# When the values of a head pair are loaded: with its first head into two buffers, or with its second into one

## The chip, the cores and the metric

The kernel runs on one core of one Trainium2 chip. The metric is the device time of one execution in microseconds (us), and the figure that counts is the median of several executions.

## The reference, cut to what matters

Causal attention with a decay, followed by two MLPs. Four batches (B), eight heads (H), 576 positions (S), head size 64.

```python
def _attn_ref(q, k, v, f):
    log_f = np.log(np.clip(f, 0.0001, 1.0))
    cum = np.cumsum(log_f, axis=-1)
    decay = cum[:, :, :, None] - cum[:, :, None, :]
    scores = scale * np.matmul(q, k.transpose(0, 1, 3, 2))
    scores = np.where(causal, -1000000000.0, scores + decay)
    attn = np.exp(scores - np.max(scores, axis=-1, keepdims=True))
    attn = attn / (np.sum(attn, axis=-1, keepdims=True) + 1e-09)
    return np.matmul(attn, v)

x = attn_out.transpose(0, 2, 1, 3).reshape(B, S, H * D)
x = _moe_ref(x)    # layer norm, x + relu(xn @ w_ch1) @ w_ch2
out = _moe2_ref(x) # relu(x @ w_in), gate with w_spatial, @ w_out
```

## The kernel before

The positions are cut by query: queries 0 to 127 of all batches first, then 128 to 255, then 256 to 575 one batch at a time. This last kind is what the change touches: the method `attention`, called four times (batches 0 to 3), each call working through four pairs of heads (p = 0 to 3), each pair through its two heads (u = 0, 1). So there are 16 pairs, counted here 0 to 15 through the four batches. Beside this attention runs the first MLP on what earlier blocks of queries gave (lines L849 and L864, the two products of a group of 256 or 512 tokens); both share TensorE, ScalarE and VectorE. A group of the MLP starts when the attention and the norm of its block are done.

What a pair does, in the order in which the code writes it:

- `operands` (L325) for the head after the present one: on SyncE's queue a load of that head's q and k (`qk`, 448 KB, L330, three buffers) and of its decay rows (`x2z`, L338); then ScalarE and VectorE split the operands in two parts (L319, L341, L342).
- with the second head (`if u`, L608): the load of the pair's v for both heads (`vr`, 320 KB, L610), on SyncE's queue too, into one buffer (`BUFS["vr"]` is 1).
- `weights` (L344) for query tiles 2 and 3 of each head: scores on TensorE (L359), masked minimum on VectorE (L363), exponentials on ScalarE (L367), the weights in two fp16 parts (`P16`, L319 and L380), and their transposition by a DMA on SyncE's queue (L382).
- after both heads: `weights` for the last tile of both, then `parts16` (L265): `vr` becomes two fp16 parts `vp` (two buffers), a high one on ScalarE (L280) and a low one on VectorE (L281). This is called the cast below; with its end the buffer of `vr` is free.
- `values` (L578), one pair late: the transposed weights times `vp` (L586), put into `xT` and `xt` on ScalarE (L591, L592). It frees the buffer of `vp`.

At the end of a batch `xT` is stored to memory by a DMA that ScalarE's queue issues (L1347), and the norm of that block begins with the subtraction of the mean in place (L782).

The code does not run in the order in which it is written. A planner orders each engine's instructions and each queue's DMAs when the kernel is compiled: what is written earlier goes first, but where an engine would have nothing to do, the planner takes a later instruction whose inputs and buffers are there by its own estimate of the times. On the chip each queue then runs in that order; an instruction that waits holds everything behind it on its queue. The transpositions and the loads of `qk`, `x2z`, `vr` and of the MLP's raw weights are all on SyncE's one queue (SPq in the rows).

Of the kernel before, what the change touches and what calls it, by code (L numbers as in the profile page):

```python
# [25 lines left out]
TOK = 256  # L26
QW = S - 2 * P
SC = 2.0 ** 14
BUFS = dict(vr=1, vp=2, qk=3, x1=3, x2=3, PT=4, sd=3, st=6, P16=5, xt=1)
BUFS0 = dict(vr=1, qk=1, e=4, diag=2, PT=2, st=4)  # L30
BUFS1B = dict(vr=4, vp=4, qk=4, sd=4, P16=4, PT=3, st=8)
BUFS1 = dict(vr=3, vp=3, qk=3, sd=2, P16=2, PT=2, st=6)
# [43 lines left out]
def qtile(i):  # L76
    return i * P, min(S, (i + 1) * P)
# [11 lines left out]
class Kernel:  # L89
# [235 lines left out]
    def operands(self, bh):  # L325

        nc, at = self.nc, self.at
        W, C = QW, QW + S
        qk = at.tile([P, C], F32, tag="qk", name="qk", bufs=BUFS["qk"])
        nc.sync.dma_start(out=qk, in_=self.qk[bh // H, bh % H])  # L330
        x1 = at.tile([P, C], F32R, tag="x1", name="x1", bufs=BUFS["x1"])
        if not self.x2z:
            for i in range(BUFS["x2"]):
                self.x2z.append(at.tile([P, C], F32R, name=f"x2z{i}"))
# [10 lines left out]
    def weights(self, i, heads):  # L345

        nc, at, bufs, q0 = self.nc, self.at, BUFS, 2 * P
        lo, hi = qtile(i)
# [222 lines left out]
    def attention(self, b, xT, xt, middle=None):  # L571
        nc, at, bufs = self.nc, self.at, BUFS
        q0, W = 2 * P, QW
        stored = xt is None
        if stored:
            xt = at.tile([P, NP, S - 512], F32, tag="xt", name="xt", bufs=bufs["xt"])

        def values(p, vp, vsc, heads, behind=None):  # L578

            pav = self.bank("av")  # L580
            for kt in range(5):
                n0 = max(kt * P, q0) - q0
                for vi, pi in ((0, 1), (1, 0), (0, 0)):
                    for u in range(2):
                        us = slice(64 * u, 64 * u + 64)
                        ins = nc.tensor.matmul(  # L586
                            pav[us, n0:W], lhsT=vp[:, vi, kt, us], rhs=heads[u][1][:, 2 * kt + pi, n0:W],
                            start=(kt == 0 and (vi, pi) == (0, 1)), stop=(kt == 4 and (vi, pi) == (0, 0)), skip_group_check=True)
                        if behind is not None and kt == 0 and (vi, pi) == (0, 1):
                            self.after(ins, behind)  # L590
            nc.scalar.activation(xT[:, p, :], pav[:, :TOK], AF.Copy, scale=vsc)  # L591
            nc.scalar.activation(xt[:, p, :], pav[:, TOK:W], AF.Copy, scale=vsc)  # L592
            if p == 1:
                self.xs = self.mo_sum(xT)
            elif p == 2:
                nc.vector.tensor_tensor(out=self.xs, in0=self.xs, in1=xT[:, 2, :], op=ALU.add)

        late = None
        passes = self.operands(b * H)
        for p in range(NP):  # L600
            if middle and p == 2:
                middle()
            heads = []
            for u in range(2):
                heads.append((passes, at.tile([P, 10, W], F16, tag="PT", name="PT", bufs=bufs["PT"])))
                if 2 * p + u + 1 < H:
                    passes = self.operands(b * H + 2 * p + u + 1)
                if u:  # L608
                    vr = at.tile([P, 5, P], F32, tag="vr", name="vr", bufs=bufs["vr"])
                    nc.sync.dma_start(out=vr, in_=self.v[b, :, p * P : (p + 1) * P].rearrange("(t p) d -> p t d", p=P))  # L610
                yield
                for i in (2, 3):
                    done = self.weights(i, heads[u:])
                    if late and (u, i) == (1, 3):
                        yield
                        values(*late, done)
                    yield
            vp = at.tile([P, 2, 5, P], F16, tag="vp", name="vp", bufs=bufs["vp"])
            self.weights(4, heads)
            vsc = self.parts16(vr, vp[:, 0], vp[:, 1], b)  # L620
            late = p, vp, vsc, heads
            yield
        yield
        values(*late)
        yield
        if stored:
            nc.scalar.dma_start(out=self.xt_d[:, :, b, :], in_=xt)
        return self.xs
# [905 lines left out]
```

## Time and profile before

| what | value |
|---|---|
| median of 3 executions | 764.3 us (762.98 to 765.41) |
| the profiled execution | 763.16 us, its span 761.2 us |
| TensorE busy in the span | 739.7 us (97%) |
| VectorE, ScalarE busy | 590.9 us (78%), 528.8 us (69%) |
| granted TensorE clock | 1.000 (2.4 GHz) |
| load of `vr` of queries from 256 on | 16 times, 320 KB each, issued between 191.7 and 427.7 us |

The span runs from the first to the last instruction of the profile; the 2.0 us between it and the time of the same execution lie around it. All stretches are counted from the start of the span.

### The profile page before, as it was taken

To read this page: it belongs to the slowest core of one execution; us is meant where nothing else is said; L and a number is where in the kernel's file an instruction comes from. 1 tells how busy PE (TensorE), PEld (TensorE's weight loads), DVE (VectorE), ACT (ScalarE), POOL (GpSimd) and SP (SyncE) were. 2 spreads that over 40 slices of the span, in tenths; PEclk is the share of its full clock that TensorE was granted. 3 is DMA by queue.
4 is the path that set the end of the run, shared out by engine and by line. 5 is a ranking of instruction groups with operands and counts; after the bars stand their busy time and mean duration, and the time that the engine had idled before them with its cause. 6 is when DMAs were issued, how large, how long until landed. Compare 5 with 4: busy or idle time off the path is not lost.

```text
span 761.2 us, 16265 instructions
## 1 busy us (share of the span) xinstructions
PE 739.7 (97%) x5912; PEld 567.9 (75%) x5912; DVE 590.9 (78%) x1569; ACT 528.8 (69%) x1320; POOL 67.4 (9%) x102
## 2 busy tenths in 40 slices
PE   8899998999999999999999999999999999999998
PEld 6788887888888877877888888644447678768686
DVE  7899799577599989989869845689456796785854
ACT  6898699576588989879857844587346764664633
POOL 6001100013102010110110100200012000000000
PEclk9999999999999999999999999999999999999999
DMA  8978694466589998988965944831025240100101
GB/s 263 295 269 274 206 266 84 89 171 105 176 167 206 198 220 183 195 189 177 201 144 116 148 84 149 213 132 56 1 22 111 70 125 1 44 21 7 57 2 62
DMA packets 164100, 104.68 MB, mean 138 GB/s; under 512 B 106147, under 2 KB 151299, under 8 KB 164021
## 3 DMA queue, kind: packets, MB, share of 16 engines
q1 hardware_dynamic: 153032, 93.06, 50.3%
q0 software_dynamic: 5376, 5.54, 5.2%
q10 hardware_dynamic: 5612, 5.06, 2.2%
q8 instruction: 46, 0.75, 0.4%
q14 instruction: 34, 0.27, 0.1%
HBM read 64.37 MB, written 15.11 MB: 104 GB/s over the span
## 4 chain that ended last, share of the span: by engine, by line
PE 63%; DVE 11%; ACT 10%; DMA 10%; issue 4%; SPq 2%; DVEq 0%; ACTq 0%
PE ph L864 16%; PE acc L849 12%; PE pb L808 8%; PE pb L809 8%; PE pb L810 8%; DMA raw<-in_moe_w_ch_dram 3%; PE s L359 3%; PE s L849 3%; DMA vr<-in_v_dram 2%; PE av L586 2%; ACT wt L744 2%; ACT P L319 2%; DMA x_d<-xT 2%; DVE P L380 1%; DMA qk<-decay 1%
## 5 line engine op out<-in xcount | busy, mean ns | idle before, releaser
L849 PE MATMUL acc<-hh,wt 128*128 128x256 f16 (+2 forms) x960 | 196.8, 295 | 3.2 <-ACT hh L875 3.2
L864 PE MATMUL ph<-xh,wt 128*128 128x256 f16 (+1 forms) x896 | 185.0, 288 | 2.0 <-DVE hl L879 2.0
L864 PEld LDWEIGHTS <-wt 128*128 128x128 f16 x1344 | 126.9, 98 | 47.4 <-issue 10.2
L849 PEld LDWEIGHTS <-wt 128*128 128x128 f16 x1344 | 128.7, 98 | 44.3 <-issue 5.3
L864 PE MATMUL ph<-xl,wt 128*128 128x256 f16 (+1 forms) x448 | 129.0, 288 | 0.0
L849 PE MATMUL acc<-hl,wt 128*128 128x256 f16 (+1 forms) x416 | 115.8, 281 | 1.1 <-DVE hl L879 1.1
L875 ACT ACTIVATE hh<-ph 128x256 f16<-128x256 f32 (+2 forms) x128 | 50.9, 397 | 45.8 <-PE ph L864 45.5
L879 DVE SCALAR_TENSOR_TENSOR hl<-ph,hh 128x256 f16<-128x256 f32 (+1 forms) x112 | 50.5, 453 | 35.9 <-ACT hh L875 35.7
L319 ACT ACTIVATE P<-sd,st 128x512 f16<-128x512 f32 (+2 forms) x128 | 70.6, 585 | 9.8 <-DVE st L370 6.9
L380 DVE SCALAR_TENSOR_TENSOR P<-sd,st,P 128x384 f16<-128x384 f32 (+2 forms) x96 | 59.2, 634 | 10.5 <-ACT P L319 10.3
L367 ACT ACTIVATE sd<-sd,st 128x384 f32<-128x384 f32 (+2 forms) x80 | 54.6, 682 | 14.4 <-DVE st L363 14.2
L359 PE MATMUL s<-x2z 128*128 128x384 f32 (+3 forms) x128 | 47.8, 382 | 1.9 <-DMA x2z<-decay_d 1.7
L363 DVE CUSTOM_DVE_ANT_0 sd<-s,mask 128x384 f32<-128x384 f32 (+2 forms) x80 | 46.0, 579 | 3.7 <-PE s L359 2.7
L900 POOL DMA_DIRECT2D x_d<-t x36 | 31.9, 1024 | 182.7 <-DVE t L896 153.1
L359 PE MATMUL s<-x 128*128 128x384 f32 (+3 forms) x128 | 41.4, 333 | 0.0
L809 PE MATMUL pb<-wsl,vh 128*128 128x288 f16 x128 | 36.6, 286 | 0.0
L808 PE MATMUL pb<-wsh,vl 128*128 128x288 f16 x128 | 36.6, 286 | 0.0
L810 PE MATMUL pb<-wsh,vh 128*128 128x288 f16 x128 | 36.4, 286 | 0.0
L810 PE MATMUL pb<-gh,woh 128*128 128x288 f16 x128 | 35.0, 286 | 0.0
L809 PE MATMUL pb<-gl,woh 128*128 128x288 f16 x128 | 35.0, 286 | 0.0
L808 PE MATMUL pb<-gh,wol 128*128 128x288 f16 x128 | 33.3, 286 | 0.0
L922 ACT ACTIVATE gh<-u 128x288 f16<-128x288 f32 x32 | 14.0, 437 | 26.5 <-DVE u L1261 26.5
(341 smaller groups left out, 1692.5 us busy)
## 6 DMA issues: line engine op xcount, KB each, us to landing
raw<-in_moe_w_ch_dram SPq DMA_DIRECT2D x32, 512.0 KB
qk<-in_qk_dram SPq DMA_DIRECT2D x32, 448.0 KB
vraw<-in_v_dram SPq DMA_DIRECT2D x5, 1024.0 KB
vr<-in_v_dram SPq DMA_DIRECT2D x16, 320.0 KB
x_d<-t POOLq DMA_DIRECT2D x36, 128.0 KB, 4.3
out_dram<-o SPq DMA_DIRECT2D x32, 144.0 KB
raw<-in_moe_w_in_dram SPq DMA_DIRECT2D x8, 512.0 KB
qk<-in_qk_dram SPq DMA_DIRECT2D x16, 192.0 KB
```

What stands on the lines that cost most here:

```text
L319: self.nc.scalar.activation(out, in_, AF.Copy, scale=scale)
L359: nc.tensor.matmul(ps[: R * u + R, : c1 - c0], lhsT=x[:, lo - q0 - R * u : hi - q0], rhs=y[:, c0:c1], start=g == 0, stop=g == len(heads[u] ...
L363: nc.vector.tensor_tensor_reduce(out=sd[:M, c0:c1], in0=ps[:M, : c1 - c0], in1=mask, scale=-0.125, scalar=3e38 if n == 0 else st[:M, n - 1 ...
L367: nc.scalar.activation(sd[:M, :N], sd[:M, :N], AF.Exp, bias=st[:M, n : n + 1], scale=-1.0, accum_out=st[:M, 2:3])
L380: low = nc.vector.scalar_tensor_tensor(out=dl, in0=src, scalar=rs, in1=dh, op0=ALU.mult, op1=ALU.subtract)
L808: first = mm(out, lhsT=al, rhs=bh, start=start, stop=False, **kw)
L809: mm(out, lhsT=ah, rhs=bl, start=False, stop=False, **kw)
L810: mm(out, lhsT=ah, rhs=bh, start=False, stop=stop, **kw)
L849: ins = nc.tensor.matmul(acc[m], lhsT=a, rhs=b, start=bank not in clear, stop=last and e == len(terms) - 1, skip_group_check=True)
L864: ins = nc.tensor.matmul(ph, lhsT=a, rhs=b, start=k == e == 0, stop=k == NK - 1 and e == len(terms) - 1)
L875: relu = nc.scalar.activation(hh, ph, AF.Relu)
L879: nc.vector.scalar_tensor_tensor(out=hl, in0=ph, scalar=0.0, in1=hh, op0=ALU.max, op1=ALU.subtract)
```

## The change

The load of a pair's v is written with the pair's first head (u = 0) instead of its second, and the tile `vr` of this kind of attention has two buffers of 2,560 bytes per partition instead of one. The load itself, its size, its queue and what reads it stay as they are.

```diff
-BUFS = dict(vr=1, vp=2, qk=3, x1=3, x2=3, PT=4, sd=3, st=6, P16=5, xt=1)
+BUFS = dict(vr=2, vp=2, qk=3, x1=3, x2=3, PT=4, sd=3, st=6, P16=5, xt=1)
...
                 if 2 * p + u + 1 < H:
                     passes = self.operands(b * H + 2 * p + u + 1)
-                if u:
+                if not u:
                     vr = at.tile([P, 5, P], F32, tag="vr", name="vr", bufs=bufs["vr"])
                     nc.sync.dma_start(out=vr, in_=self.v[b, :, p * P : (p + 1) * P].rearrange("(t p) d -> p t d", p=P))
                 yield
```

## Rows read from the trace of the kernel before

**Rows 1.** The page, part 1: busy time, share of the span, instructions of each engine.
```profile
PE 739.7 (97%) x5912; PEld 567.9 (75%) x5912; DVE 590.9 (78%) x1569; ACT 528.8 (69%) x1320; POOL 67.4 (9%) x102
```
**Rows 2.** Stretches: length, then PE, PEld, DVE, ACT, POOL busy, clock, DMA share, GB/s.
```profile
185.00:460.00 275.00, 268.49 (x2507) 222.86 (x2505) 222.27 (x602) 213.62 (x553) 27.81 (x43) 1.00 0.85 170
...
384.00:403.00 19.00, 18.94 (x173) 15.74 (x172) 11.61 (x31) 10.44 (x25) 2.54 (x3) 1.00 0.63 154
403.00:440.00 37.00, 36.88 (x343) 31.36 (x341) 32.36 (x89) 30.43 (x83) 3.92 (x6) 1.00 0.76 120
```
**Rows 3.** TensorE's waits from 185 to 460 us: total us, times, longest.
```profile
PE av L586 <- DMA PT<-P: 2.7, 2, 1.7
PE s L359 <- DMA x2z<-decay_d: 1.7, 2, 1.5
PE acc L849 <- DVE hl L879: 1.1, 1, 1.1
PE ph L864 <- DVE hl L879: 0.7, 1, 0.7
```
**Rows 4.** The chain that ended last, three stretches: start us, us, what.
```profile
208.88 3.36 DMA vr<-in_v_dram
...
269.57 3.66 DMA vr<-in_v_dram
...
273.42 4.37 DMA x_d<-xT
...
386.67 3.59 DMA vr<-in_v_dram
```
**Rows 5.** ScalarE in order of time: start us, us, instruction, [idle before <- releaser].
```profile
204.26 0.94 ACT L319 ACTIVATE x<-qk 128x896 fp32r<-128x896 f32 x1
...
212.26 0.83 ACT L280 ACTIVATE vp<-vr,vsc 128x640 f16<-128x640 f32 x1 [0.62 <-DMA vr<-in_v_dram]
...
273.25 0.83 ACT L280 ACTIVATE vp<-vr,vsc 128x640 f16<-128x640 f32 x1 [0.90 <-DMA vr<-in_v_dram]
...
390.28 0.83 ACT L280 ACTIVATE vp<-vr,vsc 128x640 f16<-128x640 f32 x1 [1.26 <-DMA vr<-in_v_dram]
```
**Rows 6.** VectorE's waits for the high half of the cast: total us, times, longest.
```profile
DVE vp L281 <- ACT vp L280: 3.7, 3, 1.9
```
**Rows 7.** VectorE in order of time, after one of these waits.
```profile
274.11 0.88 DVE L281 SCALAR_TENSOR_TENSOR vp<-vr,vsc,vp 128x640 f16<-128x640 f32 x1 [1.51 <-ACT vp L280]
```
**Rows 8.** The line of the load: issue times in ns, min/median/max, first and last start.
```profile
L610 SPq DMA_DIRECT2D vr<-in_v_dram x16: 378/532/1499, 191.7 to 427.7; - x16
```
**Rows 9.** SyncE's queue, its waits before the load: total us, times, longest.
```profile
SPq L610 <- DVE vp L281: 4.1, 3, 1.7
```
**Rows 10.** SyncE's queue in order of time: start us, us, what (merged over xcount).
```profile
190.90 0.36 SPq L330 DMA_DIRECT2D qk<-in_qk_dram  x1
...
275.02 0.38 SPq L610 DMA_DIRECT2D vr<-in_v_dram  x1
...
330.94 1.50 SPq L610 DMA_DIRECT2D vr<-in_v_dram  x1
332.53 13.64 SPq L382 DMA_TRANSPOSE PT<-P  x6
```
**Rows 11.** TensorE in order of time, where it waited for the MLP's hidden values.
```profile
218.93 0.27 PE L864 MATMUL ph<-xh,wt 128*128 128x256 f16 x1 [0.71 <-DVE hl L879]
...
301.92 0.27 PE L849 MATMUL acc<-hl,wt 128*128 128x256 f16 x1 [1.11 <-DVE hl L879]
```

## The prediction

> **What bounds the kernel now.** I began with the busy times on the page: TensorE is busy for 739.7 of the span's 761.2 us [rows 1], so all idle time of TensorE together is 21.5 us, and a change that adds and takes away no product can win only a part of it. Then the stretches: the attention that the change touches runs from 185 to 460 us, and there TensorE is busy for 268.49 of 275.00 us [rows 2], so 6.5 us of idle time lie in the reach of this change. VectorE is busy for 222 us of these 275 and ScalarE for 214 [rows 2]: they are loaded, but not the bound, since TensorE nearly always has products of the MLP to do while the attention waits for them.
>
> Third, the waits of TensorE in that stretch. They sum to 6.2 us: 2.7 for transposed weights, 1.7 for decay rows, 1.8 for the hidden values of the MLP [rows 3]. None of them names `vr` or the cast. Fourth, the chain of work that ended last: it goes through a load of `vr` three times, for 3.36, 3.66 and 3.59 us [rows 4]. This looks like 10.6 us, but a chain only tells what came last at each step, not by how much. By how much is in ScalarE's order of time: the cast stood idle for `vr` at 212.26, 273.25 and 390.28, for 0.62, 0.90 and 1.26 us [rows 5]. That is 2.78 us in 3 of 16 casts; the other 13 found their data there. VectorE waited 3.7 us for the high half in the same three places [rows 6].
>
> Why the load is late there can be read from the queue. With one buffer, a load can go out only when the cast before it has been read to the end: the load at 275.02 [rows 10] follows the low half that runs from 274.11 for 0.88 us [rows 7], by 0.03 us. SyncE's queue stood for 4.1 us in three places on that release [rows 9]. The cast in turn waits for a buffer of `vp`, which `values` of two pairs before frees. Where two `values` follow each other closely, as at the end of a batch, the next cast is due sooner than the 3.4 to 3.7 us [rows 4] that a load takes.
>
> **The change, part by part.**
>
> *Nothing is added or removed as work.* The same 16 loads of 320 KB are issued, at 0.38 to 1.50 us of SyncE's queue each, median 0.53 [rows 8]; no cast, product or transposition is added.
>
> *The second buffer.* A load now needs the end of the cast two pairs back, not one. A pair takes (460 - 185) / 16 = 17 us on average, so a load can go out about that much sooner, against 3.7 us that it takes. I take the three stalls as gone: 2.78 us of ScalarE, 3.7 us of VectorE, and on SyncE's queue part of the 4.1 us, since the load after next may stand in the same place on the queue and wait for a cast that is itself earlier by the stall.
>
> *What of it reaches TensorE.* This is the sum, and it is taken place by place from TensorE's own idle time.
> - First stall (0.62 us on ScalarE at 212.26): 6.7 us later TensorE waits 0.71 us for the hidden values of the MLP from VectorE [rows 11], and the chain comes to it through this cast. Between 0 and 0.71; I take 0.6, the stall's size.
> - Second (0.90 us at 273.25): ScalarE's queue also issues the store of `xT` behind this cast, at 273.42 [rows 4], and the norm waits for that store. The next wait of TensorE for hidden values is 1.11 us at 301.92 [rows 11], 28 us later, with other work and loads in between. Between 0 and 0.90; I take 0.4, a little under the middle.
> - Third (1.26 us at 390.28): the longest, but from 384 to 403 us TensorE is idle for 0.06 us, and from 403 to 440 for 0.12 [rows 2]. The products of the MLP hide it. Between 0 and 0.18; I take 0.15. If that cover were gone it would cost its 1.26 us.
>
> Sum 1.15 us, bounds 0 and 1.8.
>
> *What the moved load passes.* On SyncE's queue it now stands before the next head's load of `qk` and its decay rows, and before the first two transpositions of its pair. At the start of the stage it passes the third load of `qk`, issued at 190.90 [rows 10], where `vr` followed at 191.7 [rows 8]. That `qk` is 0.4 us later on the queue and at most 3.7 us later in memory; the split that reads it runs at 204.26 [rows 5], 13.4 us after the issue, which hides it. Without that cover it would cost up to 4.1 us. Later in the stage the loads stand where a cast ends in both kernels, so I cost the passing at 0. Its other end: at 330.94 one issue took 1.50 us and the six transpositions behind it 13.64 [rows 10], and TensorE's waits for transpositions and decay rows are 4.4 us today [rows 3]; if they doubled, 4.4 us are lost.
>
> *The planner.* The order of every engine is made anew with other release times, and the trace of before can't show the new order. It is bounded below by TensorE's idle time in the stage, 6.5 us to be won [rows 2], and above I use the doubling just priced. I take 0 as the middle of both.
>
> *A rule weighed.* The rows say that a buffer too few costs 2.78 us of ScalarE and little of TensorE. The Trainium skill, Perfetto Trace Analysis, section Optimization Strategy, says that a gap which repeats on the engine that should be saturated can mean that memory for the next tile ran out. Here the gap that repeats is ScalarE's, in 3 of 16 places, and not that of the saturated engine; by the rule alone one would count all 2.78 us as won.
>
> *And one that speaks against the change.* The rows show that loads of `vr` share SyncE's queue with the transpositions [rows 10]. The Trainium skill, DMA: Bandwidth & Descriptors, section Queues, rings and completion order, says that each DMA engine takes the descriptors of a ring in their order. By it a load put ahead of a transposition holds it for the whole transfer; the trace shows no case where that alone can be read off, and the sum by it is that of the slower rival below.
>
> **The sum.** On the profiled execution, 763.16 - 1.15 = 762.0 us. The median of the runs is 764.3, 1.1 us above it, and the forecast is for such a median: 764.3 - 1.2 = 763.1 us. Without the three terms' middle values it lies between 762.5 and 764.3. Less than 0.3%, 2.3 us, can hardly be told from no change, so this counts as the same.
>
> **The rivals.**
>
> *The attention gets ahead, and other waits go too.* If the three stalls at the seams of the batches are what makes the transpositions late afterwards, some of TensorE's 6.2 us of waits go with them. For it: the chain passes all three stalls, and the second holds the store and the norm. Against it: the waits for transpositions and decay rows stand at other places, and the queue before them waits for VectorE's weights, not for `vr`. All of them gone gives 764.3 - 6.2 = 758.1 us; half, 761.2. It decides from 2.3 / 6.2 = 37% of the waits on.
>
> *Slower: the earlier load in front of the transpositions.* The place is SyncE's queue in the two middle batches, as at 330.94, where the load and what stood behind it were slow [rows 10]. If loads meet the transpositions at such moments more often, TensorE's waits for them and for decay rows double: 764.3 + 4.4 = 768.7 us. It decides when two more loads fall so, each at the 1.5 us of the longest wait of today [rows 3]. For it: DMA share 0.85 over the whole stage [rows 2]. Against it: the number of bytes and issues is unchanged, and TensorE has cover in most places.
>
> *The change doesn't do what it says.* The planner may put the cast as early as its own estimate lets `vr` land, and the cast waits again: 764.3 us. Against it: a cast also needs its buffer of `vp`, which the change leaves as it is.
>
> **How the numbers follow.** Stalls gone, 0 to 1.8 us won: 0.36, the likeliest. Stalls remain in another place: 0.06, also no measurable difference. Other waits go too, over 2.3 us won: 0.33, wide because the new order can fall well. Earlier loads or a worse order, over 2.3 us lost: 0.25. So faster 0.33, same 0.42, slower 0.25. The likeliest case has the range 762.5 to 764.3; for 8 in 10 it reaches to both sides' ends, 758.1 and 768.7, since each side has more than 2 in 10. I expect no more than 2 in 10 beyond.
>
> **What would show it.** Right: no wait of a cast for `vr`; loads of `vr` issued at least 10 us ahead of their cast; SyncE's waits before the load under 4.1 us; TensorE's idle time from 185 to 460 us between 4.7 and 6.5 us; its waits for hidden values under 1.8 us. Wrong, on the fast side: waits for transpositions and decay rows well under 4.4 us. Wrong, on the slow side: the same waits above 6.7 us, or a new wait of TensorE, behind transpositions that stand just after a load of `vr`. The forecast falls altogether if time moves outside of 185 to 460 us, where none of its steps lies.

## The result

The changed kernel took 769.8 us in the median of 15 runs, the kernel before 765.35 in 15 runs beside them: ratio 1.0068, 95% interval 1.0046 to 1.0089. The forecast was no measurable change, 763.1 us. The profiled execution took 767.93 us with a span of 766.2, which is 5.0 us more than the span before. A lower clock is not the difference: taking only executions with a mean granted clock of 0.998 or more, the medians are 768.4 us (8 of the 15) and, for the kernel before, timed beside the experiments, 763.6 us (74 of 109).

The page's first part again, for the changed kernel:

```profile
PE 740.6 (97%) x5912; PEld 568.6 (74%) x5912; DVE 591.7 (77%) x1569; ACT 529.2 (69%) x1320; POOL 67.7 (9%) x102
```

Against [rows 1] each engine has the same count and almost the same busy time, so the 5 us are waiting. Where, the stretches tell. The columns are those of [rows 2]; first the changed kernel, the whole attention and then three parts of it:

```profile
185.00:460.00 275.00, 264.22 (x2448) 219.14 (x2446) 221.22 (x598) 212.59 (x548) 27.55 (x42) 1.00 0.86 169
...
185.00:279.00 94.00, 91.35 (x844) 74.99 (x843) 72.87 (x194) 72.68 (x185) 8.39 (x13) 1.00 0.86 189
279.00:317.00 38.00, 33.03 (x298) 26.57 (x297) 33.55 (x93) 30.60 (x79) 6.11 (x8) 1.00 0.98 169
317.00:460.00 143.00, 139.84 (x1310) 117.57 (x1308) 114.80 (x312) 109.31 (x285) 13.05 (x21) 1.00 0.83 157
```

and the kernel before, with its middle cut where TensorE has done nearly as many products:

```profile
279.00:312.00 33.00, 31.85 (x293) 26.06 (x292) 31.00 (x86) 30.11 (x78) 6.35 (x8) 1.00 0.98 175
312.00:460.00 148.00, 145.03 (x1365) 120.99 (x1363) 115.86 (x315) 110.02 (x286) 13.21 (x21) 1.00 0.80 152
```

TensorE's idle time is length less busy time: 10.78 us from 185 to 460 instead of 6.51 [rows 2]. The middle alone has 4.97 instead of 1.15, which is 3.8 of the 4.3 us more. It needs 38 us for 298 products where the kernel before does 293 in 33. Behind it the two kernels idle alike, 3.16 and 2.97 us.

TensorE's waits from 185 to 460 us, without two small ones, to be read against [rows 3]:

```profile
PE s L359 <- DMA x2z<-decay_d: 3.8, 3, 1.5
PE ph L864 <- DVE hl L879: 2.4, 2, 1.5
PE s L359 <- DVE st L363: 2.3, 3, 1.1
PE s L359 <- DVE x2z L342: 1.1, 1, 1.1
PE av L586 <- DMA PT<-P: 0.4, 1, 0.4
```

Waits for transposed weights fell from 2.7 to 0.4 us. Those for decay rows rose from 1.7 to 3.8, and a kind appeared that [rows 3] has not at all: scores (`s`) that wait for VectorE, 3.4 us. Most of that is in the middle, as TensorE's order of time shows (only rows with idle time):

```profile
282.61 0.27 PE L864 MATMUL ph<-xh,wt 128*128 128x256 f16 x1 [1.47 <-DVE hl L879]
...
303.53 0.47 PE L359 MATMUL s<-x2z 128*128 128x512 f32 x1 [1.07 <-DVE st L363]
306.96 0.41 PE L359 MATMUL s<-x2z 128*128 128x384 f32 x1 [1.13 <-DVE x2z L342]
...
309.57 0.50 PE L359 MATMUL s<-x2z 128*128 128x512 f32 x1 [0.94 <-DVE st L363]
```

The casts did what was forecast. Two of the three places of [rows 5] are the second and the sixth cast; here they are in ScalarE's order of time, without idle time ahead of them, and no wait of ScalarE names `vr` any more:

```profile
208.70 0.82 ACT L280 ACTIVATE vp<-vr,vsc 128x640 f16<-128x640 f32 x1
...
273.93 0.82 ACT L280 ACTIVATE vp<-vr,vsc 128x640 f16<-128x640 f32 x1
```

Two other things are new. The chain goes through the store of `xT` (issued by ScalarE's queue at the end of a batch) for 19.2 us in three places, where before it was the 4.37 us of [rows 4] and 3.56 us at 390.34, and through no load of `vr`:

```profile
197.26 6.09 DMA x_d<-xT
...
273.86 6.83 DMA x_d<-xT
...
336.42 6.24 DMA x_d<-xT
```

VectorE subtracts the mean in place in that tile (L782), so it waits for the store. The profile names the store for 8.4 us of these waits in three places from 185 to 460 us, where the kernel before waited 2.7. A fourth is put down to a product:

```profile
342.78 1.41 DVE L782 TENSOR_TENSOR xT<-xT,av 128x256 f32<-128x256 f32 x4 [2.01 <-PE acc L849]
```

But it ends 0.12 us behind the landing of the third store above (336.42 and 6.24 us), as in the kernel before the subtraction at 277.91 started 0.12 us behind its store. So it is 10.4 us in four places; from here on these waits are counted so.

And the first load now stands ahead of a load of `qk` in SyncE's queue and waits 6.3 us there for a product of the stage before (L555), whose memory, it seems, its buffer takes over:

```profile
SPq L610 <- PE av L555: 6.3, 1, 6.3
```

### The profile page after: what moved, and what is told of

Its sections match the earlier page's. It is cut to its first block, busy times and chain, and to the rows that moved or that the text cites. A ratio compares the mean times of both kernels' runs of the same rounds, so it can differ in the third digit from the quotient of the medians.

```text
span 766.2 us, 16258 instructions
## 1 busy us (share of the span) xinstructions
PE 740.6 (97%) x5912; PEld 568.6 (74%) x5912; DVE 591.7 (77%) x1569; ACT 529.2 (69%) x1320; POOL 67.7 (9%) x102
## 4 chain that ended last, share of the span: by engine, by line
PE 68%; DVE 11%; ACT 9%; DMA 8%; issue 3%; SPq 1%; ACTq 0%; DVEq 0%
PE ph L864 16%; PE acc L849 14%; PE pb L808 8%; PE pb L810 8%; PE pb L809 8%; DMA x_d<-xT 3%; PE s L359 3%; PE av L586 2%; PE s L849 1%; DVE sd L363 1%; ACT P L319 1%; DVE P L380 1%; DMA raw<-in_moe_w_in_dram 1%; ACT wt L744 1%; DMA x2z<-decay_d 1%
## 5 line engine op out<-in xcount | busy, mean ns | idle before, releaser
L367 ACT ACTIVATE sd<-sd,st 128x512 f32<-128x512 f32 (+2 forms) x80 | 54.7, 684 | 12.3 <-DVE st L363 11.8
L363 DVE CUSTOM_DVE_ANT_0 sd<-s,mask 128x384 f32<-128x384 f32 (+2 forms) x80 | 45.8, 578 | 1.2 <-PE s L359 0.5
```

The lines of the kernel that those rows point to most:

```text
L363: nc.vector.tensor_tensor_reduce(out=sd[:M, c0:c1], in0=ps[:M, : c1 - c0], in1=mask, scale=-0.125, scalar=3e38 if n == 0 else st[:M, n - 1 ...
L367: nc.scalar.activation(sd[:M, :N], sd[:M, :N], AF.Exp, bias=st[:M, n : n + 1], scale=-1.0, accum_out=st[:M, 2:3])
```

## The experiments

All ratios are to the kernel before, timed beside it on the same chip, with 95% intervals.

**Each half of the change alone.** Three theories stood at first. A: the second buffer gives every engine a new order, and this order is worse. B: the first load, which stops SyncE's queue for 6.3 us, makes `qk` late. C: earlier loads hold up the transpositions behind them. Planned alone, two buffers give the new order of TensorE to the last instruction, and of VectorE and ScalarE to all but a few; the move alone gives a third order.

```diff
 buffers_only                       move_only
-BUFS = dict(vr=1, ...              -                if u:
+BUFS = dict(vr=2, ...              +                if not u:
```

> Two buffers, the load still written with the second head. The planner gives TensorE, POOL and the other loads of SyncE's queue the very order of the changed kernel, and ScalarE and VectorE all but four instructions of it; only the first, second and fourth load of vr stand a few places later on SyncE's queue, so that the first no longer stops it for 6.4 us. Theory A (the new order of the engines, which the second buffer makes, costs the time): ratio to before 1.005 to 1.009. Theory B (the first load, which stops SyncE's queue at 190 us, costs it): 0.997 to 1.002. Theory C (loads that go out a pair earlier hold the queue and the rings for the transpositions): 1.004 to 1.008, as for A, since 12 of 16 loads stand where they stand in the changed kernel.

> One buffer, the load written with the first head. The planner makes a third order, as far from that of before as from that of the changed kernel (1460 of 5604 products of TensorE stand elsewhere). The single buffer still ties each load to the end of the cast before. Theory A: the time is that of another order and can fall on either side, 0.995 to 1.010. Theory B: the first load again stands before the third load of qk, so some of the loss, 1.003 to 1.008, if it waits at 190 us. Theory C: no loss, 0.998 to 1.002, since the loads stay late.

Two buffers alone: 1.0067 (1.0041 to 1.0093). The move alone: 1.0093 (1.0071 to 1.0115). In the first, no load stops SyncE's queue ahead of `qk` and the subtraction at the first seam does not wait, and it is as slow as the whole change, with the same three waits for scores. So B is not the cause. C finds no support either: TensorE's waits for transposed weights are 0.7 us there and 0.4 in the change, less than the 2.7 of before. The move alone loses by waits of its own, the longest 3.82 us at 322 us.

**Order and loads crossed.** From here on each engine's queue is written out: a plan lists all its instructions in the order of one kernel, and neighbours are tied by an edge that orders them and waits for nothing else. No run has this tying alone, so what it costs by itself is not shown; the run with the held queue below, which has it too, took 1.0012. The 16 loads of v stand at given places of SyncE's queue (the number of other transfers ahead of them).

```diff
+    for e, deltas in plan.items():
+        ...
+        if e == "SP" and PLACES:
+            for n, p in reversed(list(enumerate(PLACES))):
+                line.insert(p, loads[n])
+        for a, b in zip(line, line[1:]):
+            tc.add_manual_dep(b, a.name, dep, reason="order")
 places before: 122 125 129 145 159 169 172 189 196 205 212 227 236 247 248 268
 places after:  120 122 124 125 145 158 168 172 189 195 209 213 229 236 247 249
```

> The changed kernel's two buffers and its 16 loads at the changed kernel's places on SyncE's queue, and every other instruction of every engine and queue held in the order of before. Theory A: the forecast of the prediction holds, since its mechanism stands alone here: ratio 0.997 to 1.001, no cast waits for vr, TensorE idle from 185 to 460 us under 6.5 us. Theory B: the first load still stops the queue for about 6 us, 1.004 to 1.008. Theory C: 1.004 to 1.008.

> One buffer and the load with the second head, at the places that the loads have on SyncE's queue before, and every other instruction held in the order of the changed kernel. Theory A: slower as the changed kernel or more, since casts can also wait for their loads in this order: 1.005 to 1.012. Theories B and C: no loss, 0.998 to 1.003, since the loads are those of before.

1.0085 (1.0066 to 1.0104) and 1.012 (1.0094 to 1.0146). Neither says what it was built to say, since each mixture made a wait that neither kernel has. In the first, the third and fourth loads stood in SyncE's queue for 3.5 and about 4 us, waiting for casts that come later in this order, and TensorE waited 3.7 us at 220 us. In the second, the second cast waited 6.4 us for a load that its single buffer let go too late.

**The loads placed so that they don't stop the queue.** Theory D: an early load that goes out with the store of `xT` makes the store late, and VectorE's subtraction with it. Four kernels: in the order of before, each load a pair early (same traffic at the same points); all loads at the places of before (only the buffer is new); in the new order, six loads put behind the stores; in the order of before, all loads shortly ahead of their casts.

```diff
 order_before_loads_pair_ahead: 122 122 125 129 145 159 169 172 189 196 205 212 227 236 247 248
 order_before_loads_bplace:     the places of before
 order_after_loads_late:        120 122 124 125 145 158 179 183 189 195 217 222 229 236 256 258
 order_before_loads_late:       122 122 133 145 151 157 178 186 194 199 218 225 236 240 257 259
```

> Every engine and every other transfer in the order of the kernel before, two buffers for vr; each pair's load of v stands in SyncE's queue where the load of the pair before it stood (the first two together where the first stood). So there are as many loads at the same points as before, each a pair early, and no cast should wait for one. Theory A (the change loses by the new order of the engines, and the loads as such gain what the prediction took): 762 to 763 us, ratio 0.996 to 0.999, no wait of a cast for vr. Theory D (early loads lose where they share the transfers' time with the store of xT at the end of a batch, for which VectorE's subtraction of the mean waits): the bytes beside the stores are those of before, so about the same, 0.996 to 1.000. The rival that the stalls were never on TensorE's path: 0.999 to 1.001 with the stalls gone. Above 1.003 would say that early loads cost something by themselves even in the order of before.

> Every engine and every transfer, the loads of v too, in the order of the kernel before; only the second buffer for vr is there, and with it the other places that tiles get in memory. A control: all theories expect 0.998 to 1.002, with the casts of the second pairs still waiting 0.6 to 1.3 us for their loads. If it is above 1.003, the placement of tiles in memory (which tile waits for which tile of the stage before) costs time, and no theory so far has it.

> The changed kernel with every engine and every other transfer in its own order; only six loads of v (the 7th, 8th, 11th, 12th, 15th and 16th) stand later in SyncE's queue, behind the store of xT that they met, about 10 us ahead of their casts. Theory D (loads beside the stores make VectorE's subtraction of the mean wait): the wait for the stores in the three seams falls from 8.4 us by 2 or more, and the time falls to 1.001 to 1.004. Theory A (the new order as such): the waits for the stores may fall but the waits of TensorE at 303 to 313 us stay, and the ratio remains at 1.005 to 1.008.

> Every engine and every other transfer in the order of the kernel before, two buffers for vr, each load of v some 9 to 16 us ahead of its cast and none within the time of a store of xT. Theory D (loads beside the stores cost time): the waits for the stores fall below those of before, 0.994 to 0.998. Theory A (the order alone): 0.997 to 0.999, as with the loads a pair ahead. The rival that the casts' stalls were never on TensorE's path: 0.999 to 1.001.

Measured: a pair early 1.0024 (0.9999 to 1.0049); at the places of before 1.004 (1.0018 to 1.0062); new order with late loads 1.0073 (1.0047 to 1.0099); order of before with late loads 1.0053 (1.0029 to 1.0078).

The first is the forecast's own mechanism without a new order: no cast waits for `vr`. It shows no gain. Its profiled execution is not a typical one: it took 770.85 us, 5.2 above the median of its runs, with a granted clock of 0.66 from 120 to 130 us and of 0.83 from 270 to 280. TensorE's waits for the MLP's hidden values, which [rows 11] showed and the forecast hoped to shorten by 0.6 and 0.4 us, are still there:

```profile
225.15 0.27 PE L864 MATMUL ph<-xh,wt 128*128 128x256 f16 x1 [1.54 <-DVE hl L879]
...
309.76 0.27 PE L849 MATMUL acc<-hl,wt 128*128 128x256 f16 x1 [0.96 <-DVE hl L879]
```

They were 0.71 and 1.11 us. So waits of this size come without the casts' stalls.

The third run was to take the waits of theory D away and hardly did: the subtraction's waits for the store are 9.5 us in four places instead of 10.4, and the time stays, so it decides nothing on D. The fourth missed what D expected: 3.8 us of these waits, not less than the 2.7 of before, and a longer time. It has a store of 7.11 us at 272.57 with no load of v within 10 us of it, so a load isn't the only thing that can stand in its way.

The second was a control, and lost. Only the buffer is new in it, so the loads no longer wait in SyncE's queue for the cast before. Three of its casts still wait for `vr`, 3.2 us in all; the run with each load a pair early has none of this and took 0.16% less, but the two intervals overlap. The control's chain and SyncE's queue around the seam:

```profile
273.27 6.29 DMA x_d<-xT
```

```profile
272.63 0.59 SPq L610 DMA_DIRECT2D vr<-in_v_dram  x1
275.53 7.85 SPq L382 DMA_TRANSPOSE PT<-P  x4
```

In the kernel before, the single buffer held this load until 275.02 [rows 10], behind the store's issue at 273.42 [rows 4]. Here it goes out 0.64 us ahead of the store, and the store takes 6.29 us, not 4.37.

**The queue held as one buffer held it.** Theory E made a point of that: the wait on the single buffer was a brake, which let the store go first. To try it, the wait alone is put back (two buffers, nothing moved); then the wait alone is taken out of the kernel before; then SyncE's queue is held in the new order, for the casts or for the stores.

```diff
 two_buffers_queue_held (order and places of before, two buffers)
+    for later, n in [(loads[6], 5), (loads[14], 13)]:
+        tc.add_manual_dep(later, casts[n].name, held, reason="held")
 one_buffer_queue_free (one buffer): loads[6] at place 178, not 172; loads[14] at 257, not 248
 order_after_queue_held:    [(rest[171], casts 5), (rest[247], casts 13)]
 order_after_behind_stores: [(rest[171], store 4), (rest[212], store 5), (rest[248], store 6)]
```

> Two buffers for vr, every engine, every other transfer and every load of v in the order of the kernel before (the kernel that took 1.004), and one thing more: the 7th and the 15th load of v wait in SyncE's queue for VectorE's cast of the pair before, as the single buffer made them wait 1.8 us each. Theory E (the single buffer's wait held back the transpositions that stand behind it in SyncE's queue, and so let the store of xT land first, for which VectorE's subtraction waits; two buffers take that brake away): the subtraction's wait at about 280 us falls from 2.2 to under 1 us, and the ratio to 0.998 to 1.002. The rival that the second buffer's place in memory costs the time: it stays at 1.003 to 1.005.

> The kernel before with its one buffer and its order; only the 7th and the 15th load of v stand later in SyncE's queue (6 and 9 transfers later), where they no longer hold it for the cast of the pair before. Theory E (the brake): 1.002 to 1.005, the subtraction of the mean at about 280 us waits 1.5 us or more for the store. The rival that the second buffer's place in memory is the cause: 0.998 to 1.002, for no tile has moved.

> The changed kernel in its own order; two transpositions in SyncE's queue (the ones behind the 7th load and ahead of the 15th) wait for VectorE's cast of the 6th and the 14th pair, and hold what is behind them, as the single buffer held it before. Theory E (the brake): the wait of the subtraction at about 281 and 399 us falls by a microsecond or more each, ratio 1.001 to 1.004. Theory A (the new order of the engines): 1.005 to 1.008, as the change.

> The changed kernel in its own order; in each of the three seams one transposition in SyncE's queue waits until the store of xT has landed, and holds what is behind it. Theory E: the subtraction's three waits fall from 8.4 us to 3 or less, and the time with them, 1.000 to 1.003, if what is held isn't itself missed. The rival that held transpositions only move the wait to TensorE (PT): 1.005 or above with waits for PT above 3 us. Theory A (the order as such): 1.005 to 1.008 though the subtraction's waits fall.

Held in the order of before: 1.0012 (0.9995 to 1.003), from 1.004 (1.0018 to 1.0062). Nothing but two waits was added, so by the ratios these two waits are worth about 0.3%, though the intervals overlap. The second buffer's place in memory, the same in both kernels, can't cost more than the 0.3% at which this interval ends. The load goes out at 274.20, behind the store's issue at 272.60, and VectorE's wait for the store is shorter at both held places, here in this kernel and then in the one without the hold:

```profile
278.04 1.42 DVE L782 TENSOR_TENSOR xT<-xT,av 128x256 f32<-128x256 f32 x4 [1.24 <-DMA x_d<-xT]
...
394.59 1.42 DVE L782 TENSOR_TENSOR xT<-xT,av 128x256 f32<-128x256 f32 x4 [0.17 <-DMA x_d<-xT]
```

```profile
279.69 1.41 DVE L782 TENSOR_TENSOR xT<-xT,av 128x256 f32<-128x256 f32 x4 [2.21 <-DMA x_d<-xT]
...
396.58 1.41 DVE L782 TENSOR_TENSOR xT<-xT,av 128x256 f32<-128x256 f32 x4 [2.05 <-PE s L359]
```

The last of these is put down to a product, but starts 0.13 us behind the landing of a store that the chain has (391.90 and 4.55 us). In all four places the waits for the store fall from 7.4 to 4.9 us. E had expected under 1 us at 280; it is 1.24.

One buffer with the queue free: 1.0025 (1.0001 to 1.0049). The time is at the lower end of what E expected, the mechanism isn't: the subtraction waited 0.6 us for the store at 277 us, not 1.5, and 2.8 us in all, about as in the kernel before. No load went out just ahead of the store, for the load was moved away. So E holds at this place only in a narrower form: what counts is whether a load goes out ahead of the store, and not that transpositions behind it are held. What makes this run slower, if it is slower, is open.

In the new order the holds are worth nothing that can be measured: 1.0076 (1.0048 to 1.0105) and 1.0078 (1.0059 to 1.0097), though the second brought the subtraction's waits for the store down from 10.4 to 7.1 us (3 or less was expected). It has a new wait of TensorE for ScalarE of 2.0 us; that this ate the gain is not shown. Both point to the order itself for the larger part.

**One stretch of the order exchanged.** Theory F names the stretch: the middle, where TensorE has 3.8 of its 4.3 us more. On each engine there are points up to which both orders have done the same instructions; cut at two of them, at about 270 and 311 us of the kernel before, an order can be put together from both.

```diff
+C1 = {'PE': 1850, 'Activation': 457, 'DVE': 518, 'SP': 171, 'Pool': 50}    # about 270 us
+C2 = {'PE': 2228, 'Activation': 533, 'DVE': 604, 'SP': 195, 'Pool': 63}    # about 311 us
 order_after_middle_before: after up to C1, before up to C2, then after (two buffers, places of after)
 order_before_middle_after: two_buffers_queue_held, but after from C1 to C2
 order_after_end_before:    after up to C2, then before
 order_after_vector_middle: after; VectorE alone before from C1 to C2
```

> The changed kernel in its own order, but between the two points at 270 and 311 us of the kernel before every engine follows the order of the kernel before. Theory F (the new order loses in this stretch, where VectorE's four evictions of the MLP's output stand ahead of the last splits and of the scores, and TensorE waits 3.4 us for scores at 303 to 310 us): 1.001 to 1.004, TensorE's waits for scores behind VectorE in the stretch under 1 us. The rival that the loss is spread over all stretches: 1.005 to 1.007.

> The kernel with two buffers, the order of the kernel before and SyncE's queue held as by one buffer (1.0012 so far), but between the two points at 270 and 311 us every engine follows the new order. Theory F: 1.004 to 1.006, with TensorE's waits for scores behind VectorE of 3 us. The rival that the loss is spread: 1.001 to 1.003.

> The changed kernel in its own order up to the point at 311 us of the kernel before, and in the order of the kernel before from there on. Theory F: the loss is made by then, 1.005 to 1.008. The rival that it is made later or spread: 1.002 to 1.004.

> The changed kernel in its own order, but VectorE alone follows the order of the kernel before between the two points at 270 and 311 us. If VectorE's order (evictions ahead of splits) is what loses there: 1.002 to 1.004. If it is the order of TensorE's work against VectorE's, this mixture does no better than the change, 1.006 or above.

The change without its middle: 1.0035 (1.0016 to 1.0055). The middle alone, in a kernel that took 1.0012 without it: 1.0075 (1.0051 to 1.0099). The end exchanged instead: 1.0086 (1.0062 to 1.0111), no better than the change. So by the ratios the middle of the new order costs 0.33% one way and 0.63% the other, 2.5 and 4.8 us, around the 3.8 us of idle time in the trace. The second difference is clear of the noise; in the first the intervals of the two kernels overlap. The middle brings the three waits for scores with it. TensorE's order of time in the kernel that has only the middle from the new order:

```profile
302.38 0.47 PE L359 MATMUL s<-x2z 128*128 128x512 f32 x1 [1.05 <-DVE st L363]
305.81 0.41 PE L359 MATMUL s<-x2z 128*128 128x384 f32 x1 [1.13 <-DVE x2z L342]
...
308.41 0.50 PE L359 MATMUL s<-x2z 128*128 128x512 f32 x1 [0.94 <-DVE st L363]
```

In the change without its middle they are gone; TensorE's waits from 270 to 320 us there:

```profile
PE av L586 <- DMA PT<-P: 1.2, 1, 1.2
PE acc L849 <- DVE hl L879: 1.1, 1, 1.1
PE s L359 <- DMA x2z<-decay_d: 1.1, 1, 1.1
```

That is 3.3 us of idle time from 270 to 320 us; the changed kernel has 5.15 and the kernel before 1.15. From 185 to 460 us, though, it still has 10.2 us in this execution, which took 768.94 us, 2.9 above the median of its runs. So the trace shows the scores' waits gone, and not the whole of the gain.

The same two kernels speak against theory D as the main account. VectorE's waits for the store from 185 to 460 us, in the change without its middle (1.0035) and then in the kernel with the middle alone (1.0075):

```profile
DVE xT L782 <- DMA x_d<-xT: 11.7, 4, 4.6
```

```profile
DVE xT L782 <- DMA x_d<-xT: 3.0, 3, 1.9
```

The kernel that waits longer for the store is the faster one, in the ratios and in these two executions (768.94 and 770.95 us).

What the order looks like there is seen on VectorE. The norm's last product (L802) frees the four splits (L828) that feed the MLP's next tile; the four evictions of the tile before (L896) come in between or after. VectorE in the changed kernel, its other work and two of the splits left out:

```profile
297.72 1.21 DVE L802 TENSOR_TENSOR xT<-xT,y 128x1024 f32<-128x1024 f32 x1
...
299.59 0.46 DVE L828 SCALAR_TENSOR_TENSOR xl<-xT,gs,xh 128x256 f16<-128x256 f32 x1
...
301.35 0.87 DVE L896 TENSOR_SCALAR t<-acc,und 128x256 f32<-128x256 f32 x2
...
303.70 0.87 DVE L896 TENSOR_SCALAR t<-acc,und 128x256 f32<-128x256 f32 x2
...
306.63 0.47 DVE L828 SCALAR_TENSOR_TENSOR xl<-xT,gs,xh 128x256 f16<-128x256 f32 x1
```

and in the kernel before:

```profile
292.70 1.20 DVE L802 TENSOR_TENSOR xT<-xT,y 128x1024 f32<-128x1024 f32 x1
...
296.33 1.27 DVE L828 SCALAR_TENSOR_TENSOR xl<-xT,gs,xh 128x256 f16<-128x256 f32 x3
...
297.95 0.47 DVE L828 SCALAR_TENSOR_TENSOR xl<-xT,gs,xh 128x256 f16<-128x256 f32 x1
...
302.73 0.85 DVE L896 TENSOR_SCALAR t<-acc,und 128x256 f32<-128x256 f32 x2
```

From the end of L802 to the end of the last split it is 4.5 us before (293.90 to 298.42) and 8.2 after (298.93 to 307.10). Of the 3.7 us more, 1.7 are the four evictions of the MLP's output, 1.2 a head's operands (L341, L342), which come behind the last split in the kernel before, and 0.6 a gap. But for this gap VectorE runs on without a pause in that time in both kernels, so what is put ahead of the splits and of the scores' masked minimum (L363) makes them later by about its own length.

That VectorE's order *alone* does it was the fourth run, and it can't be said: 1.0199 (1.0175 to 1.0224). With the other engines left in the new order, TensorE waited 7.56 us for hidden values at 306.96. The orders of the engines fit each other, and a part of one can't be exchanged by itself.

**Both repairs, and a try at a faster kernel.** The middle of before and the held queue together; and the kernel before with the one load that met a store at 330 us [rows 10] put behind it.

```diff
 order_middle_before_queue_held: order_after_middle_before and the holds of order_after_queue_held
 one_buffer_load_11_late (one buffer, order of before): loads[10] at place 218, not 212
```

> The changed kernel with both repairs: between the points at 270 and 311 us every engine in the order of before, and two transpositions in SyncE's queue held for the casts as the single buffer held it. If the two are the whole loss: 0.999 to 1.002. If holding the queue is worth nothing outside the order of before, as in the run with the held queue in the new order: 1.003 to 1.005.

> The kernel before, one buffer, its order; only the 11th load of v stands six transfers later in SyncE's queue, behind the store of xT at 330 us that it met, and about 9 us ahead of its cast. If the store's wait there (2.1 us of VectorE) reaches TensorE: 0.997 to 0.999. If VectorE makes it up ahead of TensorE's next wait: 0.999 to 1.001.

Both repairs: 1.0019 (0.9993 to 1.0044), no longer to be told from the kernel before. Its interval overlaps that of the change without its middle, so it isn't shown that the two effects add up in this order.

The late load: 1.0039 (1.0013 to 1.0065), slower. The store at 328 us still took its time (VectorE waited 2.04 us for it; 2.1 before), so the load was not what held it up. And I had put the load directly ahead of decay rows that TensorE waits for. The chain shows it:

```profile
345.75 0.58 SPq L610 DMA_DIRECT2D vr<-in_v_dram  x1
...
346.41 3.02 DMA x2z<-decay_d
...
349.57 1.83 PE s L359 x4
```

TensorE's wait for these rows is 3.11 us here and was 1.49, the longest for decay rows in [rows 3]: 1.6 us for one load in the wrong place, about half of the 0.39% lost. No run beat the kernel before.

## Why the prediction was wrong

- **The second buffer ends the stalls: right.** No cast waits for `vr`; loads go out 9 to 43 us ahead of their casts. "At least 10 us" was missed by 0.9 us once, at the first. SyncE's waits before the load did not fall below 4.1 us: the first load alone waits 6.3.
- **1.15 us of it reach TensorE: not borne out, no gain shows.** With no stall and the order of before the ratio is 1.0024 (0.9999 to 1.0049), and the forecast was 0.9984 (763.1 of 764.3). The waits of 0.71 and 1.11 us were put down to the stalls because they came later on the chain. Without the stalls they are 1.54 and 0.96 us, in an execution with a lowered clock. A gain of about 1 us with a loss of as much or more beside it is not excluded. To count all 2.78 us, as the forecast read a rule of the Trainium skill (Perfetto Trace Analysis, Optimization Strategy), would have been further off; what the rule says is of the engine that should be saturated, and ScalarE is not that one here.
- **Passing costs 0: wrong in what was looked at.** The first `qk` was covered, as said: no wait of TensorE for it, in spite of 6.3 us in the queue. Transpositions were watched as the victims and got better (2.7 to 0.4 us). Missed was the store of `xT` on ScalarE's queue, which shares the transfers' time with SyncE's. At 273 us, where a load goes out ahead of it, the store takes 6.29 us instead of 4.37, and the single buffer's wait, costed only as a stall, had kept the load behind the store. Two such waits put back alone took the ratio from 1.004 to 1.0012, with intervals that overlap.
- **The planner's new order costs 0: this is the step that failed.** The text said that the trace of before can't show the new order, bounded it by -6.5 and +4.4 us, and took 0 as the middle; the middle of the two is a gain of 1 us, so the 0 had no reason of its own. The order came with the second buffer alone, before any load was moved (1.0067), and its middle stretch costs 2.5 to 4.8 us by exchange and 3.8 us by idle time. TensorE's idle time from 185 to 460 us is 10.8 us, where 4.7 to 6.5 was to show the forecast right.
- **The slower rival had the size by luck, and not the mechanism.** It forecast 4.4 us more from waits for transpositions and decay rows, which together went from 4.4 to 4.2 us; measured are 4.45 us more, and the new waits of the trace are 3.4 us for scores behind VectorE. Its place, "SyncE's queue in the two middle batches", has the time right and the engine wrong. The 769.8 us lie above the 768.7 at which the range for 8 in 10 ends.
- **Time moves inside 185 to 460 us: right.**

Open: why the middle is worth 0.33% one way and 0.63% the other; the rest of 1.0035; what longer waits for the store cost in the new order; why the kernel before with its queue free is at 1.0025; and which of VectorE's instructions would have to stand elsewhere, since VectorE's order couldn't be exchanged by itself.

## What to carry to other kernels

Where a planner makes the order from release times, a second buffer can be a new order for every engine before it is anything else: forecast its worth from the gaps that the order leaves, not from the stall that it ends, and pin the old order to see the two apart. A wait in a queue may be what keeps a large transfer behind a more urgent one: before removing it, look for transfers of other queues that go out in its time, and for who waits for them. An idle gap that follows a stall on the chain isn't for that reason caused by it; take the stall away alone and see.

## What the runs showed of the hardware

**A store waits for what another queue has already given out.** The store's own queue (q10, ScalarE's) and SyncE's (q1) share the 16 DMA engines. In 4.2 us from the store's issue, the kernel with two buffers at the places of before moved this:

```profile
q1 hardware_dynamic: 1605, 1.16, 111.7%
```

and the kernel before, from its own store's issue:

```profile
q1 hardware_dynamic: 996, 0.79, 62.6%
q10 hardware_dynamic: 942, 0.63, 46.8%
```

(packets, MB, share.) The difference on q1 is 0.37 MB, about one load of v, and in the first kernel not a packet of the store had begun. The Trainium skill, DMA: Bandwidth & Descriptors, section Queues, rings and completion order, says that each DMA engine takes packets from the queues that have work in turn; by that the store would have begun beside the load. The trace shows otherwise here: the store's first packets moved at about 277.5 us, when SyncE's had all but stopped (0.15 MB in the half microsecond before 277.5, 0.03 in the next), and in the kernel before at 275.8. Where SyncE's queue was nearly empty, behind the issue at 390.34 in the kernel before, they moved after 0.9 us. Why the queues did not take turns is not shown.

**The granted clock fell after a wait of TensorE, in some executions.** In the kernel with the move alone TensorE waited 3.82 us until 322.14, and the stretches read:

```profile
310.00:320.00 10.00, 8.32 (x71) 6.75 (x69) 8.83 (x27) 8.64 (x24) 0.20 (x1) 1.00 1.07 156
320.00:330.00 10.00, 7.86 (x56) 5.62 (x57) 4.79 (x15) 4.61 (x15) 0.20 (x1) 0.66 0.87 195
330.00:340.00 10.00, 10.00 (x96) 7.86 (x93) 8.80 (x21) 9.55 (x26) 0.00 (x0) 1.00 0.82 197
```

A mean of 0.66 is a mixture of the two levels, 1.2 and 2.4 GHz. So a wait can cost more than its length. In the changed kernel's own profile the three waits for scores left the clock at 1.00; in the profile of the two buffers alone, which has the same three, it was 0.66 from 310 to 320 us.
